# Ten rows of matmuls on a constant tile, put between TensorE's steps in the head of a linear-attention and two-stage expert kernel

## The chip, the cores and the metric

The kernel runs on one core of a Trainium2 chip. The metric is the device time of one execution in microseconds (us). The kernel before took 744.25 us, the median of three executions (742.01 to 744.28).

## The reference: what is computed

Three stages follow one another. First comes a linear attention over q, k, v of shape (8, 8, 576, 64):

```python
q_s = softmax(q, axis=-1)          # over the 64 columns of a head
k_s = softmax(k, axis=2)           # over the 576 positions
kv  = einsum('bhsd,bhse->bhde', k_s, v)
x   = einsum('bhsd,bhde->bhse', q_s, kv)       # then 4608 tokens of 512
h   = x @ w_in;  g = h / (1 + exp(-h));  x = g @ w_out
logits = x @ phi                    # 32 slots
slot_input = softmax(logits, axis=0).T @ x
slot_out   = 8 small two-layer networks on 4 slots each
out        = softmax(logits, axis=1) @ slot_out
```

Inputs are float32 here or are brought to it. The second line group has a hidden size of 2048, the last networks one of 1024.

## The kernel before

The 4608 tokens are cut into 18 chunks of 256. For each chunk the kernel builds x (tiles `x`, `x_mm`, lines 331 to 354), multiplies it with `w_in` in eight steps of 48 matmuls (`gemm1`, line 432, tiles `h`), forms the gated hidden tile (`act_u`) and gathers logits and slot sums. Each float32 product is made of a high and a low half: three matmuls on float32r operands replace one.

The work of the four compute engines is set out by hand. Strings of step names, `START` for the head, `CHUNK` for the middle and `END` for the tail, are played by `play`: each name runs one piece of a generator up to its next `yield`, and the instructions issued there go to the end of the queue of their engine. An engine works through its queue strictly in that order. The steps that matter here are `lq` and `qs` (loading and softmax of q: VectorE reduces a row, a matmul with the constant `swap` exchanges halves, VectorE reads the product, lines 276 to 304), `km`, `kT`, `ks`, `ke` and `kv` (the softmax of k and the products k·v: reduce, transpose on TensorE, lines 193 to 210, broadcast by a matmul with `ones`, tile `mb`, line 222, subtract, exponent, 20 matmuls, line 241), `w` and `p` (turning the loaded weights into float32 and its halves; VectorE at lines 387 and 388, VectorE or GpSimd at line 161), and `qT` and `x`. A star after a name hands a piece from GpSimd to VectorE.

TensorE's small products go to PSUM tiles with the tag `ps`, four buffers used in turn (pool `ps_s`). The tiles with tag `u0` come from the pool `cv_p` with six buffers. Two constants matter: `ident`, the identity, built by GpSimd at the start, and `swap`, which VectorE copies out of it (lines 711 and 712).

Of the kernel before, what the change touches and what calls it, by code (L numbers as in the profile page):

```python
# [8 lines left out]
F32 = mybir.dt.float32  # L9
F32R = mybir.dt.float32r  # L10
# [10 lines left out]


START = """
lq.0 lk.0.0 qs.0 qs.0 qs.0 qs.0 km.0 kT.0 qs.0 kT.0 kT.0 qs.0 lk.1.0 lw.0 km.1 qs.0 ks.0 kT.1 qs.0 w.0 ks.0
qs.0 kT.1 ke.0 qT.0.0 kT.1 lw.1 ks.1 qT.0.0 qT.0.0 w.1 w.0 w.0 ks.1 lphi lk.0.1 lk.1.1 lw.2 kv.0 qT.0.1 ke.1
w.1 w.0 lq.1 kv.1 w.2 qT.0.1 w.1 kv.0 w.0* qs.1 qT.0.1 w.1 kv.0 lw.3 lk.3.0 w.1 w.2 qs.1 lw.4 qs.1 kv.0 kv.1
w.2 kv.1 w.3 kv.1 km.3 kT.3 w.3 x.0.0 qs.1 w.2 x.0.1 x.0.0 w.4 w.3 w.2 x.0.1 kT.3 kT.3* x.0.0 lw.5 qs.1 w.3
w.4 lp.0 w.5 x.0.1 ks.3 qs.1 w.4 h.0.0 ks.3 w.3 w.5 h.0.1 qs.1 w.4 h.0.0 h.0.0 qs.1 w.4* w.5 h.0.2 qs.1 p.0
h.0.1 w.5 lp.1 lk.3.1 p.1 h.0.2 ke.3 lw.6 p.0 h.0.3 w.5 qT.1.0 h.0.1 h.0.4 p.0 lw.7 p.0 p.1 h.0.2 w.6 w.6 p.1
lp.2 qT.1.0 w.7 h.0.4 h.0.3 p.0 w.7 kv.3 p.1 h.0.5 qT.1.0 w.6 p.0 x.1.0 w.6 p.1 qT.1.1 p.1 h.0.3 h.0.4 p.0 p.1  # L30
w.7 kv.3 w.6* h.0.5 qT.1.1 w.7 x.1.0 l.0.1 h.0.6 lk.2.0 p.2 km.2 qT.1.1 x.1.0 p.2 kT.2 w.7 h.0.5 h.0.7 x.1.1
lp.3 p.2 kT.2 kT.2 p.2 kv.3 h.0.6 p.3 h.0.7 x.1.1 p.3 x.1.1 h.0.6 p.2 lp.4 lk.2.1 p.2 h.1.0 ks.2 p.4 lp.5 lq.2
h.0.7 kv.3 p.3 p.3 lp.6 p.4 p.5 p.3 h.1.0 p.4 p.5 h.1.1 p.3 h.1.2 qs.2 p.2 p.4 qs.2 ks.2 p.6 p.4 lp.7 p.3 qs.2
p.5 ke.2 l.0.3 p.4 h.1.0 p.5 h.1.1 p.5 p.7 qs.2 p.6 h.1.3 h.1.2 qs.2 h.1.3 p.6 h.1.1 p.4 p.7 p.5 kv.2 kv.2
p.7* h.1.4 p.6 p.5 qs.2 p.6* h.1.2 p.7 l.0.5 qs.2 p.6 h.1.5 qs.2 qs.2 p.7* kv.2 h.1.4 h.1.3 p.6 rg.0 p.7 h.1.6
p.7 qT.2.0 l.0.7 kv.2 h.1.4 h.1.5 qT.2.0 rg.0 qT.2.0 x.2.0 dl.0 x.2.0 dl.0 qT.2.1 h.1.5 rg.0 qT.2.1 qT.2.1
h.1.7 ds.0 ds.0 x.2.0 ds.0 x.2.1 l.1.1 dT.0 l.1.3 rg.0 x.2.1 h.1.7 h.1.6 dT.0 x.2.1 h.1.6 dg.0 dg.0 h.1.7 lq.3
lk.4.0 lk.4.1 l.1.5
"""
CHUNK = """  # L40
qs rg km h.0 h.0 o h.1 qs e.7 rg h.1 dl kT o h.0 kT sc sc kT* dl qs qs* h.1 h.2 rg ks ds h.3 ks ds qs h.2 h.3
# [22 lines left out]
def kernel(  # L64
# [19 lines left out]
    nc = tc.nc  # L84
# [3 lines left out]
    NS = phi.shape[1]  # L88
    E, F = w1.shape[1], 2 * w1.shape[3] // (phi.shape[0] // 128)
    SPE = NS // E  # L90
    P = 128
    CH = 256
# [23 lines left out]
    ident = const.tile([P, P], F32, name="ident")  # L116
# [13 lines left out]
    def ps(shape, name):  # L130
        cnt[0] += 1
        return ps_s.tile(shape, F32, tag="ps", name=f"{name}_{cnt[0]}")


    def right(name, bufs):
        st = ExitStack()
        return st.enter_context(tc.tile_pool(name=name, bufs=bufs, side="right")), st
# [12 lines left out]
    cv_p, cv_st = right("cv_p", 3)  # L150
# [158 lines left out]
    def warm_up(n, at):  # L309
        t = ps([P, P], "warm")  # L310
        for _ in range(n):
            nc.tensor.matmul(t, ident, ident, start=True, stop=True)


    def q_trans(c, half):
# [46 lines left out]
    def load_piece(kind, j):  # L362
        if j % 2 == 0:
            pool = {"w2": gb_p, "p0": gk_p, "p2": gk_p, "p6": gk_p}.get(f"{kind}{j}", ga_p)
            t = pool.tile([P, 2, KD * 256], w_in.dtype, tag="g", name=f"raw_{kind}{j}")
            for i in range(2):
                raw[kind, j + i] = t[:, i].rearrange("p (k f) -> p k f", k=KD)
        src = w_in if kind == "w" else w_out_t
        nc.sync.dma_start(raw[kind, j], src[j])
# [218 lines left out]
    def one(f):  # L588
        def g(*a):
            f(*a)  # L590
            return
            yield
        return g
# [61 lines left out]
    def close(st, n):  # L655
        st.close()
        give_slots(n)

    parts = {
        "wu": one(warm_up), "lq": one(load_q), "lk": one(kv_dma), "lphi": one(phi_dma),  # L660
        "lw": one(lambda j: load_piece("w", j)), "lp": one(lambda j: load_piece("p", j)),
        "km": one(kv_max), "kT": kv_maxT, "ks": kv_sub, "ke": one(kv_exp), "kv": kv_mm,
        "qs": q_soft, "qT": q_trans, "x": x_mm, "w": conv_w, "p": conv_p,
# [118 lines left out]
    for ft in range(KF):  # L782
        g = ft % G
        nc.tensor.matmul(psi[NS * g:NS * g + NS, :], aT[:, ft, :], w_t[ft // 4][:, ft % 4, :],
                         start=(ft < G), stop=(ft >= KF - G))
# [95 lines left out]
    for e in range(E):  # L881
        layer2(1, e)
        n = NCH * (e + 1) // E
# [59 lines left out]
```

## Time and profile before

| what | us |
|---|---|
| three executions | 742.01, 744.25, 744.28 |
| span of the profiled execution, first to last instruction | 741.5 |
| what an execution adds around the span (fastest and slowest run less the span) | 0.5 to 2.8 |
| TensorE busy in the span | 674.9 |
| VectorE busy in the span | 569.3 |
| ScalarE and GpSimd busy | 285.7 and 154.2 |

The profile gives the span of the profiled execution and no other time for it. Averages hide that the program has stages: in the first hundred microseconds VectorE is the busy engine and TensorE has gaps, later it is the other way round. Busy time of TensorE counts overlapping matmuls once, and the ends of matmuls are modelled; the distance between two starts is the safer price. A wait is read from the idle time in front of an instruction and from what ended it. The granted clock is a share of full speed: 1.00 is 2.4 GHz, 0.50 is 1.2 GHz.

### The profile page before, as it was taken

Reading aid. Unit: us, or ns where it says so; the run is one execution under the profiler, and the core shown is the slowest. Engines: PE = TensorE matmul, PEld = TensorE weight load, DVE = VectorE, ACT = ScalarE, POOL = GpSimd, SP = SyncE. Lnnn points to the kernel's source line nnn. Section 1 sums busy time; section 2 is a strip of 40 time slices with the busy share of each in tenths; the row PEclk is TensorE's granted clock in tenths of the full one; section 3 lists DMA queues with packets and bytes.
Section 4 is the critical chain, followed back from the end, with each engine's and each line's share of the span. In section 5 each row is a group of like instructions: output and inputs, shape, how many; then the busy total and the mean of one; then the engine's idle time right before and its main releaser. Section 6 shows DMA issues by size and latency. Waiting matters only on the chain.

```text
span 741.5 us, 15214 instructions
## 1 busy us (share of the span) xinstructions
PE 674.9 (91%) x6214; PEld 574.7 (77%) x6214; DVE 569.3 (77%) x998; ACT 285.7 (39%) x512; POOL 154.2 (21%) x108
## 2 busy tenths in 40 slices
PE   1347699999999999999999999999999999998993
PEld 1247588889897987989798898989898998893452
DVE  8999999788887979798888778878896784334253
ACT  3466564233444344333434334242433323322223
POOL 4857564011202111122112111010201000003000
PEclk9759799999999999999999999999999999999998
DMA  8623733665565739374765626845351747799998
GB/s 344 276 108 114 304 138 79 187 192 122 161 151 168 199 117 234 99 223 96 204 158 170 143 60 183 264 136 129 102 114 41 217 93 242 265 357 374 369 374 340
DMA packets 39509, 141.73 MB, mean 191 GB/s; under 512 B 6672, under 2 KB 6672, under 8 KB 30736
## 3 DMA queue, kind: packets, MB, share of 16 engines
q1 hardware_dynamic: 39440, 140.76, 60.4%
q8 instruction: 49, 0.80, 0.5%
q14 instruction: 20, 0.16, 0.1%
HBM read 93.55 MB, written 13.63 MB: 145 GB/s over the span
## 4 chain that ended last, share of the span: by engine, by line
PE 71%; DVE 17%; SPq 3%; issue 3%; ACT 2%; DMA 2%; POOL 0%; DVEq 0%; POOLq 0%; ACTq 0%
PE h L432 45%; PE sg L554 5%; PE pl L481 5%; SPq L491 3%; PE l L833 2%; DMA gk<-gT 2%; PE l L806 2%; PE kv L241 2%; DVE mg_p L388 2%; DVE mg_w L388 1%; PE x L348 1%; PE x L349 1%; DVE u L445 1%; PE x L347 1%; PE po L855 1%
## 5 line engine op out<-in xcount | busy, mean ns | idle before, releaser
L432 PE MATMUL h<-x,win_hi 128*128 128x256 f32 x2304 | 432.4, 289 | 5.0 <-DVE u L445 4.1
L432 PEld LDWEIGHTS h<-x,win_hi 128*128 128x128 f32 x2304 | 362.3, 194 | 32.7 <-issue 30.4
L432 PE MATMUL h<-x,win_lo 128*128 128x256 f32 x1152 | 328.1, 285 | 2.0 <-DVE win_lo L161 2.0
L432 PEld LDWEIGHTS h<-x,win_lo 128*128 128x128 f32 x1152 | 222.9, 193 | 2.3 <-DVE win_lo L161 2.3
L443 ACT ACTIVATE u<-h 128x512 f32<-128x512 f32 x144 | 85.5, 596 | 181.6 <-PE h L432 175.7
L445 DVE SCALAR_TENSOR_TENSOR u<-u,h 128x512 f32<-128x512 f32 x144 | 97.1, 674 | 51.0 <-ACT u L443 50.9
L452 DVE STREAM_TRANSPOSE gT<-u 128x512 f32<-128x512 f32 x128 | 91.1, 712 | 4.5
L161 POOL TENSOR_TENSOR q<-q,qsm 128x1024 f32<-128x1024 f32 x16 | 31.6, 1977 | 173.0 <-DVE qsm L303 76.8
L481 PE MATMUL pl<-u,wphi 128*32 128x256 f32 x576 | 47.5, 394 | 2.7 <-DVE wphi L419 2.7
L554 PE MATMUL sg<-gk,d 128*32 128x512 f32 x288 | 40.5, 594 | 1.8 <-DMA gk<-gT 1.4
L354 DVE TENSOR_TENSOR x<-x,x 128x512 fp32r<-128x512 f32 x36 | 24.7, 686 | 22.0 <-ACT x L352 21.5
L161 POOL TENSOR_TENSOR qlo<-q,qhi 128x512 fp32r<-128x512 f32 x17 | 22.5, 1322 | 90.6 <-ACT qhi L329 90.6
L294 ACT ACTIVATE q<-q 128x1024 f32<-128x1024 f32 x18 | 19.1, 1060 | 52.9 <-DVE q L161 48.9
L193 DVE TENSOR_REDUCE m<-kv 128x256 f32<-128x1280 f32 x16 | 39.3, 2454 | 0.0
L352 ACT CAST x<-x 128x512 fp32r<-128x512 f32 x36 | 21.0, 584 | 42.5 <-PE x L349 42.2
L161 POOL TENSOR_TENSOR mg_o<-mg_o,raw_o 128x512 f32<-128x512 f32 x16 | 20.9, 1308 | 73.3 <-DVE mg_o L388 64.8
L257 ACT CAST kvn_hi<-kvtmp 64x128 fp32r<-64x128 f32 x32 | 9.5, 296 | 51.2 <-DVE kvtmp L252 50.8
L329 ACT CAST qhi<-q 128x512 fp32r<-128x512 f32 x34 | 20.9, 615 | 18.9 <-DVE q L323 13.3
L348 PE MATMUL x<-qlo,kvn_hi 128*128 128x256 f32 (+3 forms) x96 | 27.3, 285 | 0.0
L349 PE MATMUL x<-qhi,kvn_lo 128*128 128x256 f32 (+3 forms) x96 | 27.2, 284 | 0.0
L347 PE MATMUL x<-qhi,kvn_hi 128*128 128x256 f32 (+3 forms) x96 | 27.2, 283 | 0.0
L554 PEld LDWEIGHTS sg<-gk,d 128*32 128x32 f32 x288 | 12.1, 109 | 18.7 <-issue 11.8
(155 smaller groups left out, 905.6 us busy)
## 6 DMA issues: line engine op xcount, KB each, us to landing
gk<-gT SPq DMA_DIRECT2D x256, 128.0 KB, 2.5
w<-in_moe_w_dram SPq DMA_DIRECT2D x32, 1024.0 KB, 7.5
kv<-in_kv_dram SPq DMA_DIRECT2D x16, 650.0 KB, 6.2
kv<-in_kv_dram SPq DMA_DIRECT2D x16, 640.0 KB, 4.9
q<-in_q_dram SPq DMA_DIRECT2D x18, 512.0 KB, 3.5
raw_w<-in_moe_w_in_dram SPq DMA_DIRECT2D x8, 1024.0 KB, 7.4
raw_p<-in_moe_w_out_t_dram SPq DMA_DIRECT2D x8, 1024.0 KB, 7.9
raw_o<-in_moe_w_out_dram SPq DMA_DIRECT2D x8, 1024.0 KB, 6.9
```

What stands on the lines that cost most here:

```text
L161: (nc.vector if star[0] else nc.gpsimd).tensor_tensor(*a)
L193: nc.vector.tensor_reduce(m1.rearrange("p (h d) -> p h d", h=HH), k_t[u].rearrange("p h j d -> p h d j"), axis=AX.X, op=ALU.max,)
L347: nc.tensor.matmul(o, kh, qh[:, i, p0:p1], start=True, stop=False)
L348: nc.tensor.matmul(o, kh, ql[:, i, p0:p1], start=False, stop=False)
L349: nc.tensor.matmul(o, kl, qh[:, i, p0:p1], start=False, stop=True)
L354: nc.vector.tensor_tensor(lo, px, hi.bitcast(F32), ALU.subtract)
L432: nc.tensor.matmul(ph[:, i, :], a, x[:, kk, :], start=(n == 0), stop=(n == 3 * KD - 1))
L443: nc.scalar.activation(u, ph, AF.Tanh, scale=0.5)
L445: nc.vector.scalar_tensor_tensor(u, u, 1.0, ph, ALU.add, ALU.mult)
L452: nc.vector.transpose(out=gT_t[c][:, :, 2 * s:2 * s + 2, :].rearrange("p j a f -> p a j f"), in_=u.rearrange("p a (j t) -> p a j t", t=32),)
L481: nc.tensor.matmul(pl_t[c][NS * g:NS * g + NS, :], wphi[:, ft, :], u[:, i, :], start=(ft < G), stop=(ft >= KF - G))
L554: nc.tensor.matmul(pg[NS * i:NS * i + NS, :], d[:, j, :], gk[:, j, i, :], start=(j == 0), stop=(j == TPC - 1))
```

## The change

A step `rw` (function `row`) is added. The first call fills two tiles of the tag `u0` with the identity, by eight copies on ScalarE. Every call takes two `ps` tiles and issues 16 matmuls on these constants into them; nothing reads the products. The ten rows differ in shape, and each stands once in `START`. Nothing else in the table changes its order; `CHUNK` and `END` are unchanged.

```diff
-lq.0 lk.0.0 qs.0 qs.0 qs.0 qs.0 km.0 kT.0 qs.0 kT.0 kT.0 qs.0 lk.1.0 lw.0 km.1 qs.0 ks.0 kT.1 qs.0 w.0 ks.0
+rw.0 lq.0 lk.0.0 qs.0 qs.0 qs.0 qs.0 km.0 kT.0 qs.0 rw.1 kT.0 kT.0 qs.0 lk.1.0 lw.0 km.1 qs.0 rw.2 ks.0 kT.1
...
+    shapes = {}
+
+    def row(n):
+        if not shapes:
+            for w in range(2):
+                t = cv_p.tile([P, 2, CH], F32R, tag="u0", name=f"row{w}", bufs=6)
+                for i in range(2):
+                    nc.scalar.copy(t[:, i, 0:P], ident)
+                    nc.scalar.copy(t[:, i, P:], ident)
+                shapes[w] = t
+        a, b = shapes[0], shapes[1]
+        f = a.rearrange("p i n -> p (i n)")
+        g = b.rearrange("p i n -> p (i n)")
+        o = [ps([P, 512], f"row{n}{x}") for x in range(2)]
+        mm = nc.tensor.matmul
+        for k in range(16):
+            t = o[k // 8]
+            m, w = (f, g)[k % 2], (a[:, 0, 0:P], a[:, 1, 0:P], b[:, 0, 0:P])[k % 3]
+            c = slice(NS * (k % 4), NS * (k % 4) + NS)
+            if n == 0:
+                mm(t, w, m, start=True, stop=True)
+            elif n == 1:
+                mm(t[:, 0:256], w, m[:, 0:256], start=True, stop=True)
+            elif n == 2:
+                mm(t, w, (a, b)[k % 2].rearrange("p i (x y) -> p x i y", x=2)[:, :, :, 0:P], start=True, stop=True)
+            elif n == 3:
+                mm(t[:, 0:384], w, m[:, 0:384], start=True, stop=True)
+            elif n == 4:
+                mm(t[c, :], w.bitcast(F32)[:, 0:NS], m.bitcast(F32), start=True, stop=True)
+            elif n == 5:
+                mm(t[c, 0:256], w.bitcast(F32)[:, 0:NS],
+                   m.bitcast(F32).rearrange("p (x y) -> p x y", y=64)[:, :, 0:32], start=True, stop=True)
+            elif n == 6:
+                mm(t[0:64, :], w[:, 0:64], m, start=True, stop=True)
+            elif n == 7:
+                mm(t[c, 0:256], w.bitcast(F32)[:, 0:NS], m.bitcast(F32)[:, 0:256], start=True, stop=True)
+            elif n == 8:
+                mm(t, f[:, 0:P], m, start=True, stop=True)
+            elif n == 9:
+                h = slice(64 * (k % 2), 64 * (k % 2) + 64)
+                mm(o[k % 2], w[h], m[h], start=True, stop=True)
```

On TensorE's queue the head of the kernel before begins as follows (`qmx` and `qsm` belong to `qs`, `m1T` to `kT`, `mb` to `ks`; 0 and 1 in these names are the first two halves of batch 0, and the numbers at the end count tiles).

```order
L286 MATMUL qmx_194<-qmx_192,swap 128x32
L204 MATMUL m1T_200<-ident,m_0_198 128x128 x2
L300 MATMUL qsm_222<-qsm_214,swap 128x32
L222 MATMUL mb_224<-dg_209,ones 128x256 x2
L204 MATMUL m1T_227<-ident,m_1_220 128x128 x2
L222 MATMUL mb_253<-dg_247,ones 128x256 x2
L241 MATMUL kv_270<-kv_190 64x65 x20
```

The same place in the changed kernel, with the first matmul of each row (`row` tiles; 15 more of the same shape follow each of them):

```order
L335 MATMUL row_1_198<-row_188 128x512
...
L286 MATMUL qmx_222<-qmx_220,swap 128x32
L204 MATMUL m1T_228<-ident,m_0_226 128x128 x2
L337 MATMUL row_5_232<-row_188 128x256
...
L300 MATMUL qsm_268<-qsm_260,swap 128x32
L339 MATMUL row_8_270<-row_188 128x512
...
L222 MATMUL mb_288<-dg_255,ones 128x256 x2
L204 MATMUL m1T_291<-ident,m_1_266 128x128 x2
L343 MATMUL row_12_301<-row_188 32x512
...
L350 MATMUL row_14_335<-row_188 32x256
...
L222 MATMUL mb_353<-dg_329,ones 128x256 x2
L345 MATMUL row_17_357<-row_188 32x256
...
L348 MATMUL row_19_388<-row_188 64x512
...
L241 MATMUL kv_406<-kv_218 64x65 x20
```

Every matmul of the softmax steps keeps its place among the others, and rows 0, 1, 2, 4, 7, 5 and 6 (in this order) stand in front of `qmx`, `qsm`, `mb`, `mb` and `kv`. Further down on TensorE, row 3 stands between the first and the second `kv`, and row 9 and row 8 stand as here, ahead of the first matmuls of `x`:

```order
L241 MATMUL kv_455<-kv_262 64x65 x20
L355 MATMUL row_25_491<-row_188 128x512
...
L286 MATMUL qmx_517<-qmx_487,swap 128x32
L204 MATMUL m1T_539<-ident,m_3_537 128x128 x2
L352 MATMUL row_29_544<-row_188 128x512
...
L390 MATMUL x_564<-qhi_0_325,kvn_hi_158 128x256
L391 MATMUL x_564<-qlo_0_326,kvn_hi_158 128x256
```

On ScalarE the queue of the changed kernel begins with the copies (before, it began with the table load and the exponent of q at line 294):

```order
L322 ACT_TABLE_LOAD
L322 CAST row_188<-ident 128x128
L323 CAST row_188<-ident 128x128
...
L294 ACTIVATE q_216<-q_216 128x1024
L427 ACTIVATE mg_w_296<-raw_w_264 128x1024
```

The two tiles of the tag `u0` are the first of their pool; the copies stand ahead of all other work of ScalarE.

## Rows read from the trace of the kernel before

**Rows 1.** The page: the span and the number of instructions.
```profile
span 741.5 us, 15214 instructions
```

**Rows 2.** Busy time per engine (count), granted clock, DMA share and rate, by stretch.
```profile
0.00:20.00 20.00, 3.79 (x11) 2.29 (x11) 16.78 (x38) 7.46 (x8) 10.46 (x21) 1.00 0.81 319
20.00:40.00 20.00, 5.47 (x83) 4.81 (x83) 18.41 (x21) 9.73 (x13) 15.85 (x8) 0.71 0.79 317
...
20.90:25.95 5.05, 4.48 (x81) 4.02 (x80) 4.78 (x5) 3.34 (x4) 3.17 (x2) 1.00 0.32 80
```

**Rows 3.** Pieces of the chain that ended last: start, length, engine, what.
```profile
121.30 1.14 DVE qsm L297
123.44 3.10 PE h L432 x24
...
157.44 1.32 PE kv L241 x40
...
259.30 1.72 PE sg L554 x16
```

**Rows 4.** TensorE in order of time: start, length, instruction, idle time before it.
```profile
6.69 0.64 PE L286 MATMUL qmx<-qmx,swap 128*128 128x32 f32 x2 [6.69 <-DVE qmx L283]
...
13.10 0.77 PE L222 MATMUL mb<-dg,ones 128*128 128x256 f32 x2
...
21.03 2.44 PE L241 MATMUL kv<-kv 128*64 128x65 f32 x40
...
42.66 0.41 PE L348 MATMUL x<-qlo,kvn_hi 128*128 128x256 f32 x1
...
44.80 0.41 PE L349 MATMUL x<-qhi,kvn_lo 128*128 128x256 f32 x1
```

**Rows 5.** Two stretches of `h` matmuls, columns as in Rows 2.
```profile
52.40:55.65 3.25, 3.15 (x14) 3.15 (x15) 3.25 (x4) 1.05 (x1) 3.25 (x2) 0.50 0.00 0
55.65:58.99 3.34, 3.34 (x28) 3.34 (x28) 3.31 (x3) 2.64 (x3) 1.30 (x2) 0.96 0.00 0
```

**Rows 6.** VectorE in order of time, at the instructions that need `ident` or TensorE.
```profile
1.34 2.07 DVE L711 COPY s<-ident 32x32 f32<-32x32 f32 x4 [1.34 <-POOL ident masks.py:199]
...
15.25 1.43 DVE L225 TENSOR_TENSOR kv<-kv,mb 128x1280 f32<-128x1280 f32 x1
...
21.14 1.49 DVE L225 TENSOR_TENSOR kv<-kv,mb 128x1280 f32<-128x1280 f32 x1 [0.93 <-PE mb L222]
...
25.80 0.15 DVE L249 TENSOR_SCALAR rz<-kv 128x2 f32<-128x2 f32 x1
...
34.41 0.17 DVE L288 TENSOR_TENSOR qmx<-qmx,qmx 128x32 f32<-128x32 f32 x1
...
49.30 0.68 DVE L354 TENSOR_TENSOR x<-x,x 128x512 fp32r<-128x512 f32 x1
```

**Rows 7.** ScalarE in order of time: the table load and the first cast of `x`.
```profile
4.32 1.28 ACT L294 ACT_TABLE_LOAD   x1 [4.32 <-DMA q<-in_q_dram]
...
43.97 0.59 ACT L352 CAST x<-x 128x512 fp32r<-128x512 f32 x1 [2.21 <-PE x L349]
```

**Rows 8.** Groups by line and shape: a 128x128 cast on ScalarE; busy us, mean ns.
```profile
L749 ACT CAST cc<-logit 128x128 fp32r<-128x128 f32 x1 | 0.3, 298 | 0.5 <-PE l L806 0.5
```

**Rows 9.** A GpSimd instruction, and two of VectorE, in order of time.
```profile
26.01 2.38 POOL L161 TENSOR_TENSOR mg_w<-mg_w,raw_w 128x1024 f32<-128x1024 f32 x1 [1.94 <-ACT win_hi L399]
...
26.39 3.09 DVE L161 TENSOR_TENSOR win_lo<-mg_w,win_hi 128x1024 fp32r<-128x1024 f32 x1
...
57.32 1.22 DVE L388 SCALAR_TENSOR_TENSOR mg_w<-raw_w,mg_w 128x1024 uint32<-128x1024 uint32 x1
```

**Rows 10.** VectorE's groups by line and shape, 26 to 124 us.
```profile
L388 DVE SCALAR_TENSOR_TENSOR mg_p<-raw_p,mg_p 128x1024 uint32<-128x1024 uint32 x8 | 14.0, 1754 | 0.3
L388 DVE SCALAR_TENSOR_TENSOR mg_w<-raw_w,mg_w 128x1024 uint32<-128x1024 uint32 x6 | 12.4, 2074 | 0.2
...
L161 DVE TENSOR_TENSOR win_lo<-mg_w,win_hi 128x1024 fp32r<-128x1024 f32 x3 | 8.4, 2804 | 0.0
```

More of the change, by code (lines that the diff above doesn't have):

```diff
@@ L23 @@
 START = """
-lq.0 lk.0.0 qs.0 qs.0 qs.0 qs.0 km.0 kT.0 qs.0 kT.0 kT.0 qs.0 lk.1.0 lw.0 km.1 qs.0 ks.0 kT.1 qs.0 w.0 ks.0
[L25 to L38, printed above, removed]
+rw.0 lq.0 lk.0.0 qs.0 qs.0 qs.0 qs.0 km.0 kT.0 qs.0 rw.1 kT.0 kT.0 qs.0 lk.1.0 lw.0 km.1 qs.0 rw.2 ks.0 kT.1
@@ new lines @@
+qs.0 w.0 ks.0 qs.0 rw.4 kT.1 ke.0 qT.0.0 kT.1 lw.1 rw.7 ks.1 qT.0.0 rw.5 qT.0.0 w.1 w.0 w.0 ks.1 lphi lk.0.1
+lk.1.1 lw.2 rw.6 kv.0 qT.0.1 ke.1 w.1 w.0 lq.1 rw.3 kv.1 w.2 qT.0.1 w.1 kv.0 w.0* qs.1 qT.0.1 w.1 rw.9 kv.0 lw.3
+lk.3.0 w.1 w.2 qs.1 lw.4 qs.1 kv.0 kv.1 w.2 kv.1 w.3 kv.1 km.3 kT.3 w.3 rw.8 x.0.0 qs.1 w.2 x.0.1 x.0.0 w.4 w.3
+w.2 x.0.1 kT.3 kT.3* x.0.0 lw.5 qs.1 w.3 w.4 lp.0 w.5 x.0.1 ks.3 qs.1 w.4 h.0.0 ks.3 w.3 w.5 h.0.1 qs.1 w.4
+h.0.0 h.0.0 qs.1 w.4* w.5 h.0.2 qs.1 p.0 h.0.1 w.5 lp.1 lk.3.1 p.1 h.0.2 ke.3 lw.6 p.0 h.0.3 w.5 qT.1.0 h.0.1
@@ new lines @@
+h.0.4 p.0 lw.7 p.0 p.1 h.0.2 w.6 w.6 p.1 lp.2 qT.1.0 w.7 h.0.4 h.0.3 p.0 w.7 kv.3 p.1 h.0.5 qT.1.0 w.6 p.0 x.1.0
+w.6 p.1 qT.1.1 p.1 h.0.3 h.0.4 p.0 p.1 w.7 kv.3 w.6* h.0.5 qT.1.1 w.7 x.1.0 l.0.1 h.0.6 lk.2.0 p.2 km.2 qT.1.1
+x.1.0 p.2 kT.2 w.7 h.0.5 h.0.7 x.1.1 lp.3 p.2 kT.2 kT.2 p.2 kv.3 h.0.6 p.3 h.0.7 x.1.1 p.3 x.1.1 h.0.6 p.2 lp.4
+lk.2.1 p.2 h.1.0 ks.2 p.4 lp.5 lq.2 h.0.7 kv.3 p.3 p.3 lp.6 p.4 p.5 p.3 h.1.0 p.4 p.5 h.1.1 p.3 h.1.2 qs.2 p.2
+p.4 qs.2 ks.2 p.6 p.4 lp.7 p.3 qs.2 p.5 ke.2 l.0.3 p.4 h.1.0 p.5 h.1.1 p.5 p.7 qs.2 p.6 h.1.3 h.1.2 qs.2 h.1.3
@@ L39 @@
+p.6 h.1.1 p.4 p.7 p.5 kv.2 kv.2 p.7* h.1.4 p.6 p.5 qs.2 p.6* h.1.2 p.7 l.0.5 qs.2 p.6 h.1.5 qs.2 qs.2 p.7* kv.2
+h.1.4 h.1.3 p.6 rg.0 p.7 h.1.6 p.7 qT.2.0 l.0.7 kv.2 h.1.4 h.1.5 qT.2.0 rg.0 qT.2.0 x.2.0 dl.0 x.2.0 dl.0 qT.2.1
+h.1.5 rg.0 qT.2.1 qT.2.1 h.1.7 ds.0 ds.0 x.2.0 ds.0 x.2.1 l.1.1 dT.0 l.1.3 rg.0 x.2.1 h.1.7 h.1.6 dT.0 x.2.1
+h.1.6 dg.0 dg.0 h.1.7 lq.3 lk.4.0 lk.4.1 l.1.5
 """
@@ L659 @@
     parts = {
-        "wu": one(warm_up), "lq": one(load_q), "lk": one(kv_dma), "lphi": one(phi_dma),
+        "wu": one(warm_up), "rw": one(row), "lq": one(load_q), "lk": one(kv_dma), "lphi": one(phi_dma),
         "lw": one(lambda j: load_piece("w", j)), "lp": one(lambda j: load_piece("p", j)),
```

## The prediction

> **What bounds the kernel now.** I read the busy time by stretch first. In the first 20 us VectorE is busy 16.78 us and TensorE 3.79, in the next 20 us 18.41 and 5.47 [rows 2]: the head hangs on VectorE, and TensorE has 40 − 9.26 = 30.7 us without work in it. The chain that ended last says the same: its pieces are VectorE's up to the reduce at 121.30, and from 123.44 on they are TensorE's `h` matmuls [rows 3]. So what delays VectorE in the first 123 us delays the end one for one, since behind it TensorE works without a gap. What delays TensorE alone in the head costs nothing until VectorE waits for a product. VectorE asks TensorE at few places: at 7.4 us (`qmx`, whose matmul starts at 6.69 [rows 4]), at 15.25, 21.14, 25.80, 34.41 and, by way of ScalarE's cast, at 49.30 [rows 6]. I therefore went through TensorE's queue row by row and asked at each of these places how late the product comes.
>
> **Prices of the rows.** No row's shape is in the trace; the nearest are these. A 128x256 matmul on float32r follows the last one after (44.80 − 42.66)/10 = 0.214 us at the lower clock [rows 4], and after 3.34/28 = 0.119 us at a granted clock of 0.96 [rows 5]. That is by columns, so 16 matmuls of 512 columns (rows 0, 2, 6, 8, 9) take 6.9 us at the lower level and 3.8 us at the upper, 256 columns (row 1) 3.4 and 1.9, 384 (row 3) 5.1 and 2.9. Plain float32 into 32 partitions is like `sg`: 16 records, two for each of 8 matmuls of 512 columns, in 1.72 us at the upper level [rows 3]; so 3.4 us for row 4 (6.9 at the lower level), and half of that for rows 5 and 7. Together 31 us at the upper and 57 us at the lower level: even at the upper level they fill the whole idle time of 30.7 us, so they can't all be hidden.
>
> **Which clock.** The granted clock reads 1.00 from 20.90 to 25.95 [rows 2], but the 40 matmuls of `kv` in it take 2.44 us [rows 4], where later 40 take 1.32 [rows 3]. The early reading is not what the matmuls show; I take the lower level for the start. From 52.40 the `h` matmuls ran without a gap at 0.50 until 55.65, and then at 0.96 [rows 5]; so a burst from rest is priced with half of its matmuls at each level, 8 × 0.428 + 8 × 0.239 = 5.3 us for 512 columns. From row 1 on TensorE hardly rests until row 9, and I take the upper level there.
>
> The Trainium skill (TensorE: Matmul & The Clock Gate, Part 1) says that the halved clock is the default and that activity lifts it; by that the early 1.00 is an unset reading. This trace's 2.44 us agrees. By the reading alone the first term below would be 2.1 instead of 3.6.
>
> **The sum, place by place.** All times are of the profiled execution; a delay, once there, moves everything behind it.
> - Row 0. It needs `ident` (1.34 us [rows 6]), the table load (1.28 us [rows 7]), which no longer waits for q, and eight casts of 128x128 at 0.30 us [rows 8]: ready at 5.0. With 5.3 us of matmuls TensorE is free at 10.3, where `qmx` now starts at 6.69: **+3.6**. Bounds: 3.8 us of matmuls gives +2.1, 6.9 gives +5.2. The casts themselves are hidden: ScalarE's next piece of work waits for `qmx`.
> - Row 1 stands before `qsm`, while VectorE does two reduces of k and one of q: 1.9 to 3.4 us beside them, **0** (1 at most).
> - Row 2 stands before `mb`. That matmul starts at 13.10, takes 0.77 [rows 4] and is read at 15.25 [rows 6], so 1.4 us are to spare. 3.8 us push it from 12.9 to 16.7, its end to about 17.3: **+2.0** (lower level: +5.1).
> - Rows 4 and 7, 5.1 us, stand before the second `mb`. TensorE reaches it at about 22.5 on the scale of the trace plus 3.6, ends it at 22.9, and VectorE wants it at 21.14 + 2.0: **0** (lower level +5).
> - Rows 5 and 6, 5.5 us, stand before `kv`, which takes 1.3 and some 0.2 to be seen: 29.9, wanted at 25.80 + 2.0 = 27.8: **+2.1** (lower level +8).
> - Row 3, the second `kv` and row 9 take 2.9 + 1.3 + 3.8, then `qmx` 0.65: 38.5, wanted at 34.41 + 4.1 = 38.5: **0**. If row 9's matmuls, which use 64 rows each in turn, run in pairs, 1.9 us are to spare; at the lower level +6.
> - Row 8 stands before `x`, after a rest of TensorE of some 8 us, so 5.3 us: the cast of `x` on ScalarE (0.59 us at 43.97 [rows 7]) comes at 49.3 with half a microsecond of matmul time won back at the upper level, and VectorE's line 354 wants it done at 49.30 [rows 6]. Behind the cast ScalarE has the next weight conversions, for which VectorE waits next: **+0.7** (lower level +2.7, nothing if the clock is already up).
>
> Sum: 3.6 + 2.0 + 2.1 + 0.7 = **+8.4 us** of waits on VectorE.
>
> **What comes back.** VectorE's `win_lo` takes 3.09 us from 26.39, and ends 1.1 us after a GpSimd instruction that ran from 26.01 to 28.39 [rows 9]; it was held up for 1.9 us. In the changed kernel VectorE stands at 25.80 for 2.1 us, GpSimd's instruction does not, and `win_lo` finds it finished: −1.9. More of this kind lies behind it: line 388 takes 1.22 us when nothing is in its way [rows 9], but 1.754 and 2.074 us on the mean over 14 cases, and `win_lo` 2.804 over three [rows 10]. That is 8 × 0.53 + 6 × 0.85 + 3 × 1.6 = 14.2 us of hold-ups up to 124 us. When VectorE's waits move it against GpSimd, some go and others come; I take another −0.8.
>
> The Trainium skill (SBUF — State Buffer, SBUF: two separate sides) says that VectorE and GpSimd share a pair of ports as an exclusive lock, held for the whole instruction, so the later one fully blocks. The trace's 3.09 us agrees. Without that rule the sum would stay at 8.4.
>
> Net **+5.7 us**: the span of 741.5 [rows 1] becomes 747.2, and with 0.5 to 2.8 us around it 747.7 to 750.0. Against the median of the runs, which lies 2.75 above that span, it is 744.25 + 5.7 = **750.0 us**.
>
> **DMA.** The transfer of the third half batch into the buffer of the first waits for `kv`, which ends some 8 us later than now, while the reader is some 5 us later; I see no reader that comes to wait, and price it at nothing.
>
> **Rivals.**
> - *A shape that is dearer than its columns.* Rows 2 and 5 read their moving operand in pieces, row 6 has 64 columns of weights, row 9 half of the rows. For it: no such shape is in the trace. Against it: `kv` with 64 columns and `sg` with 32 cost what their columns say. If row 2 or row 6 costs double, its 3.8 us come on top at a place where no slack is left, and row 5 another 1.7: +9 to +13, about 755 us.
> - *The clock stays at the lower level through the head.* The rests of VectorE's chain between the rows speak for it, the 31 us of rows in 30.7 us against it. The lower prices above give 5.2 + 5.1 + 5 + 8 + 6 + 2.7 = 32, less 2.7 that come back: about 773 us.
> - *Not slower: the hold-ups between VectorE and GpSimd come back in full.* Place: VectorE's lines 388 and 161 from 26 to 124 us; price: up to 14.2 us. For it: VectorE is the bound there, and each hold-up depends on who starts first. From the point at which 6.2 of the 14.2 us are saved, the sum falls below 2.2 us; with 8.4 it is zero, and with 10 it would be 742.6. Against it: most hold-ups are between instructions that feed one another, and move together.
> - *The rows cost nothing because nothing reads them.* They stand in TensorE's queue ahead of `qmx`, `mb` and `kv`, so only row 0's lateness could shrink, to +2.1; this is inside the case before.
>
> **How the numbers follow.** What a measurement of this kernel can tell from no change is 0.3%, 2.2 us. The forecast (+3 to +8.5; 747.5 to 753) has 0.68. Dearer shapes 0.13, the clock staying low 0.05. The hold-ups coming back 0.14: 0.09 of it within 2.2 us, 0.03 faster, 0.02 still slower. So slower 0.88, same 0.09, faster 0.03. The range of 745 to 758 leaves out the low clock and the far ends of the others.
>
> **What would show it.** `qmx` starts near 10.3 and not 6.69; VectorE is idle before lines 288, 225 (first) and 249 for 3 to 4, 2 and 2 us; rows 1, 4, 7, 3 and 9 end before VectorE asks. `win_lo` at 26.39 + delay takes about 1.2 us. The last VectorE piece of the chain comes at 127 instead of 121. I am wrong if one row takes over 5.5 us behind row 1, if VectorE's idle time in the head is far from 8 us, or if the same waits are seen and the `h` matmuls of the middle nevertheless start on time.

## The result and the profile after

The changed kernel takes 747.14 us, the median of eight executions (744.94 to 750.46), against 742.45 us of the kernel before, eight executions beside them (740.64 to 744.28). The ratio is 1.0062, 95% interval 1.0038 to 1.0086: 4.7 us slower. (One execution of e5 below, of 1314 us, is left out of its ratio and its median.) The profiled execution took 746.72 us, 1.8 us more than its span, which answers to [rows 1]:

```profile
span 744.9 us, 15643 instructions
```

TensorE in the head, in order of time (start, length, instruction, idle time before it). These are the first matmuls of rows 0, 1, 2, 5, 6, 9 and 8, the last three of row 0, and the products that stand behind the rows ([rows 4] has those of before).

```profile
2.97 0.79 PE L335 MATMUL row<-row 128*128 128x512 f32 x1 [2.97 <-ACT row L323]
...
8.81 0.86 PE L335 MATMUL row<-row,row 128*128 128x512 f32 x3
9.51 0.30 PE L286 MATMUL qmx<-qmx,swap 128*128 128x32 f32 x2
...
12.75 0.56 PE L337 MATMUL row<-row 128*128 128x256 f32 x1
...
15.88 0.30 PE L300 MATMUL qsm<-qsm,swap 128*128 128x32 f32 x2
16.02 0.47 PE L339 MATMUL row<-row 128*128 128x512 f32 x1
...
19.78 0.41 PE L222 MATMUL mb<-dg,ones 128*128 128x256 f32 x2
...
26.06 0.40 PE L345 MATMUL row<-row 128*32 128x256 f32 x1
...
27.93 0.45 PE L348 MATMUL row<-row 128*64 128x512 f32 x1
...
31.75 1.39 PE L241 MATMUL kv<-kv 128*64 128x65 f32 x40
...
37.40 0.49 PE L355 MATMUL row<-row 64*128 64x512 f32 x1
...
39.45 0.41 PE L286 MATMUL qmx<-qmx,swap 128*128 128x32 f32 x2
...
48.78 0.78 PE L352 MATMUL row<-row 128*128 128x512 f32 x1
...
54.44 0.28 PE L390 MATMUL x<-qhi,kvn_hi 128*128 128x256 f32 x1
```

The distance from a row's first matmul to what stands behind it (for row 5 that is row 6) is the row's price: row 0 6.5 us, row 1 3.1, row 2 3.76, row 5 1.9, row 6 3.8, row 9 2.05, row 8 5.7. The clock that goes with them, by stretch (columns as in [rows 2]):

```profile
3.00:8.40 5.40, 5.40 (x12) 3.96 (x13) 2.70 (x13) 0.72 (x4) 0.56 (x2) 1.00 1.03 416
8.40:12.00 3.60, 1.41 (x8) 1.07 (x6) 2.15 (x2) 0.00 (x0) 1.88 (x1) 0.99 0.98 401
12.00:15.00 3.00, 2.56 (x12) 2.59 (x13) 2.09 (x5) 2.90 (x3) 1.13 (x5) 0.50 1.08 423
15.00:20.00 5.00, 5.00 (x28) 4.33 (x27) 2.90 (x4) 0.37 (x1) 2.30 (x3) 0.97 0.56 230
20.00:40.00 20.00, 19.86 (x232) 12.43 (x230) 15.77 (x20) 10.78 (x12) 13.77 (x10) 1.00 0.51 190
40.00:45.00 5.00, 0.00 (x0) 0.00 (x0) 4.82 (x6) 0.05 (x1) 4.07 (x2) 0.77 1.00 423
45.00:50.00 5.00, 1.53 (x5) 1.37 (x6) 4.62 (x5) 3.74 (x5) 0.00 (x0) 0.50 0.59 245
```

Row 0's matmuls show the lower level up to about 8.4 us, whatever the reading says (its first 13 take 5.84 us, 0.45 each), and the upper one for its last three (0.23 each, from 8.81 to 9.51). TensorE then rests until 12.4 us and is at the lower level again for most of row 1. From 15 to 40 us it is at the upper level, falls back while it rests between rows 9 and 8, and has to be brought up again by row 8. VectorE, at the instructions of [rows 6] and [rows 9]:

```profile
9.85 0.19 DVE L288 TENSOR_TENSOR qmx<-qmx,qmx 128x32 f32<-128x32 f32 x1 [4.07 <-PE qmx L286]
...
20.23 1.49 DVE L225 TENSOR_TENSOR kv<-kv,mb 128x1280 f32<-128x1280 f32 x1 [2.29 <-PE mb L222]
...
26.17 1.49 DVE L225 TENSOR_TENSOR kv<-kv,mb 128x1280 f32<-128x1280 f32 x1 [1.13 <-PE mb L222]
...
33.19 0.16 DVE L249 TENSOR_SCALAR rz<-kv 128x2 f32<-128x2 f32 x1 [2.44 <-PE kv L241]
...
33.79 1.86 DVE L161 TENSOR_TENSOR win_lo<-mg_w,win_hi 128x1024 fp32r<-128x1024 f32 x1
...
39.89 0.19 DVE L288 TENSOR_TENSOR qmx<-qmx,qmx 128x32 f32<-128x32 f32 x1 [0.19 <-PE qmx L286]
40.00 4.22 DVE L260 TENSOR_TENSOR kvn_lo<-kvtmp,kvn_hi 64x128 fp32r<-64x128 f32 x2
...
55.97 0.69 DVE L397 TENSOR_TENSOR x<-x,x 128x512 fp32r<-128x512 f32 x1
```

The three waits that the prediction named are there. The first, 4.07 us, is longer than the delay that it makes: 0.73 us of it are there before the change too, and 0.9 us come from q's first reduce, which began at 4.56 us in this execution and at 5.42 us in that of before. VectorE is late by 2.5 us at the first of these instructions, by 5.0 at 20.23, still 5.0 at 26.17 (rows 4 and 7 are hidden), 7.4 at 33.19 and 6.7 at 55.97. The chain of waits then passes to TensorE ([rows 3]):

```profile
128.43 1.14 DVE qsm L297
130.58 3.10 PE h L475 x24
...
166.43 1.73 PE sg L597 x16
...
365.03 1.88 PE sg L597 x10
```

The first two pieces are 7.1 us later than before. The span is only 3.4 us longer, so 3.7 us come back between 130 us and the end. The chain of the kernel before shows where:

```profile
160.20 1.88 PE sg L554 x10
...
287.23 6.89 DMA gk<-gT
294.21 1.88 PE sg L554 x10
```

`sg` forms the slot sums of the chunk before (line 554, `slot_g`), whose operand `gk` is brought by 16 transfers, the gathers, on SyncE's queue (`regroup`). Its 8 matmuls leave 16 records. A group "x10" in this chain is one in which the last ten of them stood until a transfer had landed. The kernel before has four, at 160, 227, 294 and 362 us; the changed kernel has one, at 365 us. In the groups by line the 288 records and the idle time ahead of them read, before and after:

```profile
L554 PE MATMUL sg<-gk,d 128*32 128x512 f32 x288 | 40.5, 594 | 1.8 <-DMA gk<-gT 1.4 <-DVE d L545 0.3
```

```profile
L597 PE MATMUL sg<-gk,d 128*32 128x512 f32 x288 | 38.0, 593 | 0.4 <-DVE d L588 0.3
```

That is 42.3 against 38.4 us, 3.9 less. Between the `u` activations at 136.9 and 664.5 us of before, and the same two of the changed kernel, all other groups of matmuls agree to 0.2 us, so what comes back in the middle comes back at `sg`. To follow the delay along the run I compared the start of the same `u` activation of ScalarE (before: line 443) in each profile with that in the first profile of before. All numbers are us; the first column is the time in before, the last two are span and median.

| kernel | 137 | 194 | 261 | 363 | 665 | span | median |
|---|---|---|---|---|---|---|---|
| changed, first profile | +7.1 | +6.1 | +5.2 | +3.5 | +3.0 | +3.4 | 747.14 |
| changed, second profile (e8) | +7.9 | +6.8 | +5.6 | +4.6 | +4.4 | +5.0 | 747.54 |
| e1, hidden rows alone | +1.1 | +1.8 | +0.9 | +0.8 | +1.8 | +1.8 | 743.12 |
| e2, rows in TensorE's rests | -0.3 | -1.2 | -1.9 | -3.1 | -3.0 | -3.0 | 741.45 |
| e3, row 0 alone, 36 matmuls | +6.3 | +5.8 | +4.6 | +4.3 | +2.8 | +5.6 | 748.52 |
| e4, before again | +0.5 | +1.6 | +0.7 | +0.4 | +0.8 | +1.3 | 743.15 |
| e5, exposed rows alone | +8.1 | +7.2 | +6.6 | +5.3 | +4.2 | +4.7 | 749.94 |
| e6, before, `sg` later | 0.0 | -0.7 | -1.8 | -3.0 | -2.8 | -2.5 | 740.68 |
| e7, changed, `sg` later | +7.9 | +7.3 | +6.2 | +5.1 | +5.0 | +5.3 | 748.09 |

The kernel before ran 742.82 us beside e1 to e4 and 743.32 us beside e5 to e8 (medians of 29 and 11 executions).

### The profile page after: what moved, and what is told of

Its sections match the earlier page's. It is cut to its first block, busy times and chain, and to the rows that moved or that the text cites. A ratio compares the mean times of both kernels' runs of the same rounds, so it can differ in the third digit from the quotient of the medians.

```text
span 744.9 us, 15643 instructions
## 1 busy us (share of the span) xinstructions
PE 702.0 (94%) x6422; PEld 595.6 (80%) x6422; DVE 567.4 (76%) x998; ACT 287.1 (39%) x520; POOL 154.0 (21%) x108
## 4 chain that ended last, share of the span: by engine, by line
PE 82%; DVE 13%; ACT 2%; issue 2%; DMA 0%; SPq 0%; DVEq 0%; ACTq 0%
PE h L475 49%; PE pl L524 5%; PE sg L597 5%; PE kv L241 2%; PE l L876 2%; PE l L849 2%; DVE mg_p L431 2%; PE po L898 2%; PE x L391 1%; PE x L392 1%; PE x L390 1%; DVE mg_p L430 1%; DVE u L488 1%; PE uT L508 1%; DVE m L193 1%
## 5 line engine op out<-in xcount | busy, mean ns | idle before, releaser
L597 PE MATMUL sg<-gk,d 128*32 128x512 f32 x288 | 38.0, 593 | 0.4 <-DVE d L588 0.3
L366 DVE STREAM_TRANSPOSE q<-q 128x512 f32<-128x512 f32 x34 | 23.6, 693 | 3.4 <-POOL q L161 3.4
```

The costliest lines, as they stand in the source:

```text
L597: nc.tensor.matmul(pg[NS * i:NS * i + NS, :], d[:, j, :], gk[:, j, i, :], start=(j == 0), stop=(j == TPC - 1))
```

## The experiments

**e1: the hidden rows alone.** Rows 0, 2, 5 and 6 are without their matmuls; row 0 only fills the tiles.

```diff
-        for k in range(16):
+        for k in range(0 if n == 0 else 16):
...
-... qs.0 rw.2 ks.0 kT.1 ... qT.0.0 rw.5 qT.0.0 ... lw.2 rw.6 kv.0
+... qs.0 ks.0 kT.1 ... qT.0.0 qT.0.0 ... lw.2 kv.0
```

> Rows 1, 4, 7, 3, 9 and 8 stay where the change puts them; rows 0, 2, 5 and 6 have no matmuls, and the two constant tiles are still filled at the start. Theory (only rows that VectorE waits for cost something): the first h matmul of the PE-bound stretch, at 123.44 us before and 130.58 with all ten rows, comes at 123.5 to 126 (0 to 2.5 later; 0.7 of it for row 8, up to 1.5 if row 4 runs at the lower clock because row 2 no longer precedes it), and the time is 0 to 2.5 us above before. Rival (TensorE's total work in the head counts, wherever it stands): these six rows are 15.5 of the 30 us of matmuls, so about half of the 7.1, 3.5 us, with VectorE's idle time spread over all of its reads.

743.12 us, ratio 0.9997 [0.9979, 1.0014]. The 96 matmuls more on TensorE's queue cost nothing that can be measured. VectorE is on time to 0.1 us at the first `kv`, and 0.5 us late behind row 8. Compared with the changed kernel this puts the 4.7 us on rows 0, 2, 5 and 6. The waits at `sg` are as before (40.1 and 3.0 us, 43.1 in all).

**e2: all ten rows, moved to where TensorE rests.** The tiles are filled at the start; rows 0, 2, 5, 6 and 8 stand behind the products that they had delayed, row 4 behind the second `kv`, and row 9 ahead of the next q step.

```diff
-rw.0 lq.0 ... qs.0 rw.2 ks.0 ... rw.5 qT.0.0 ... lw.2 rw.6 kv.0 ... rw.8 x.0.0
+rw.10 lq.0 ... qs.0 ks.0 ... qT.0.0 ... lw.2 kv.0 ... rw.9 qs.1 rw.0 rw.2 rw.5 ... x.0.1 rw.6 x.0.0 ... rw.8 h.0.3
```

> All ten rows with their 160 matmuls, but row 0, 2 and 5 moved into TensorE's rest after the second qmx, row 4 behind the second kv, row 6 behind the matmuls of x and row 8 ahead of the fourth h step; rows 1, 7, 3 and 9 near their old places. Theory (place decides): the first h matmul of the PE-bound stretch comes at 123 to 125 instead of 130.58, and the time is 0 to 1.5 us above before. Rival (the amount of work counts): the same +7 us at that matmul and +4.7 us in time as with the rows in their first places.

741.45 us, ratio 0.9984 [0.9971, 0.9997]: the same 160 matmuls, and no time for them. VectorE at the same places as above:

```profile
6.50 0.19 DVE L288 TENSOR_TENSOR qmx<-qmx,qmx 128x32 f32<-128x32 f32 x1 [0.73 <-PE qmx L286]
...
25.03 0.15 DVE L249 TENSOR_SCALAR rz<-kv 128x2 f32<-128x2 f32 x1
```

The cost of the change is a matter of place, not of work. In this execution too q's first reduce began at 4.56 instead of 5.42 us, which accounts for the small lead at the start. The lead grows from 0.3 to 3.0 us in the middle, and `sg` stands at 39.2 and 0.5 us, 39.7 in all: 2.6 less than before, in a kernel whose head is not late.

**e3: a single delay at the start.** Row 0 alone, with 36 matmuls.

```diff
-        for k in range(16):
-            t = o[k // 8]
+        for k in range(36):
+            t = o[k // 18]
...
-rw.0 lq.0 ... rw.1 ... rw.2 ... rw.4 ... rw.7 ... rw.5 ... rw.6 ... rw.3 ... rw.9 ... rw.8 ...
+rw.0 lq.0 ...
```

> Only row 0, but with 36 matmuls instead of 16; no other row. TensorE is then free for the first qmx at about 14.1 us instead of 9.5, so everything behind it is moved by 7.05 us at once and nothing else is changed. Theory A (a delay of the head reaches the end one for one, and the 3.7 us that the profiled run of the change won back between 161 and 367 us were transfers that happened to come late in the profiled run of before): first h matmul of the PE-bound stretch at 130.5, time 6 to 8 us above before. Theory B (a later head is partly won back in the middle, because the gathers of gk then meet fewer other transfers): the same 130.5, but only 3 to 5 us in time. Theory C (VectorE's hold-ups against GpSimd win back part of it already in the head): first h matmul before 129.

748.52 us, ratio 1.0085 [1.0068, 1.0101], 5.7 us slower by the medians and 6.3 by the ratio. VectorE's first wait is 7.39 us, the delay there +6.65, and the first `h` of the chain starts at 129.79, +6.35: through the head a delay at the start is handed on almost whole. Behind it 3.5 us come back by 665 us, and the tail takes 2.8 again. In the last 22 us of the span TensorE's clock reads 0.64, where before it reads 0.86 (first line before, second e3):

```profile
719.50:741.50 22.00, 10.76 (x80) 7.26 (x72) 8.41 (x13) 7.80 (x15) 0.00 (x0) 0.86 0.82 337
```

```profile
725.10:747.10 22.00, 10.13 (x44) 8.12 (x42) 7.35 (x11) 7.04 (x13) 0.00 (x0) 0.64 0.73 299
```

So the total came to the lower edge of the range expected for "one for one" (6 to 8 us), but by luck: a gain in the middle and a loss in the tail nearly cancelled. As many `sg` waits went as in the changed kernel (38.1 and 0.9 us, 39.0 in all). What lowers the clock in the tail was not tried.

**e4: the kernel before again,** for a second profile.

> The kernel before, unchanged, for a second profile. Theory A (late gathers come and go by chance): the waits of sg for gk near 160, 227 and 293 us are of other sizes than the 1.0, 1.0 and 1.9 us of the first profile, and the offset against the first profile moves in steps at these places; first h matmul of the PE-bound stretch within 0.5 us of 123.44. Theory B (they belong to the kernel): the same three waits within 0.2 us. Time 742.5 us within 0.2%.

743.15 us, ratio 1.0010 [0.9999, 1.0022]. Its `sg` group reads 40.0 and 2.7 us of idle time, 42.7 in all, and its chain has late groups at 161.78, 260.95 and 362.96, not all in the chunks of the first profile. In these two executions the waits differ in their place, and hardly in their sum.

**e5: the exposed rows alone.** Rows 0, 2, 5 and 6, without the six others.

```diff
-... qs.0 rw.1 kT.0 ... qs.0 rw.4 kT.1 ... lw.1 rw.7 ks.1 ... lq.1 rw.3 kv.1 ... w.1 rw.9 kv.0 ... w.3 rw.8 x.0.0
+... qs.0 kT.0 ... qs.0 kT.1 ... lw.1 ks.1 ... lq.1 kv.1 ... w.1 kv.0 ... w.3 x.0.0
```

> The changed kernel with rows 0, 2, 5 and 6 alone, the four that delayed VectorE; rows 1, 4, 7, 3, 9 and 8 are left out. Theory A: the hidden rows did something for the others, they kept TensorE busy so that rows 2, 5 and 6 ran at the upper clock level; without them row 2 starts on a rested engine, its 16 matmuls take 5 to 7 us instead of 3.7, rows 5 and 6 together more than 5.6, and VectorE is late by 8 to 11 us after the wait for kv, where the changed kernel had +7.4. Time 748 to 751. Rival B: the price of a row does not hang on the hidden ones; the delay after kv stays at +7.4, without row 8's half microsecond the first h that TensorE sets the pace for comes 6 to 7 us late, time 746 to 747.5.

749.94 us, the median of five, ratio 1.0085 [1.0066, 1.0105]. With 96 matmuls less than the changed kernel it is not faster; by the medians it is 2.4 us slower than e8, but the two intervals against the kernel before still touch. TensorE (rows 2, 5 and 6 and the products behind them), then VectorE, then the clock:

```profile
16.05 0.77 PE L339 MATMUL row<-row 128*128 128x512 f32 x1
...
21.46 0.40 PE L222 MATMUL mb<-dg,ones 128*128 128x256 f32 x2
...
27.54 0.63 PE L345 MATMUL row<-row 128*32 128x256 f32 x1
...
31.11 0.69 PE L348 MATMUL row<-row 128*64 128x512 f32 x1
...
35.91 2.55 PE L241 MATMUL kv<-kv 128*64 128x65 f32 x80
```

```profile
21.90 1.49 DVE L225 TENSOR_TENSOR kv<-kv,mb 128x1280 f32<-128x1280 f32 x1 [3.64 <-PE mb L222]
...
37.35 0.16 DVE L249 TENSOR_SCALAR rz<-kv 128x2 f32<-128x2 f32 x1 [4.94 <-PE kv L241]
```

```profile
15.00:20.00 5.00, 4.37 (x12) 3.59 (x13) 3.23 (x4) 0.69 (x1) 2.37 (x4) 0.54 0.58 240
```

Row 2 takes 5.4 us instead of 3.76, row 5 3.6 instead of 1.9, row 6 4.8 instead of 3.8, and VectorE is late by 11.5 us at line 249, where the changed kernel has 7.4. Theory A holds: the rows that are hidden kept the clock at the upper level, and so made the exposed ones cheap. In this profiled execution most of it comes back at once, at `win_lo` (1.69 us, [rows 9] has 3.09) and the instructions behind it: the first `h` of the chain is 8.1 us late, 0.2 to 1.0 more than in the changed kernel. This execution, of 748.02 us, is the fastest of the five; it ends 0.3 us before the span of e8, so where the others lose the 2.4 us was not seen. What e5 shows is the delay at `kv`, not a time that is longer beyond doubt.

**e6 and e7: `sg` one `h` step later,** in the kernel before and in the changed one. In the strings `sg` is the first `dg` of a chunk. An `h` step is 24 matmuls (`x24` in the chain), some 3 us: not 48 matmuls, as said of `gemm1` above, and not the 16 of 1.9 us of the expectation.

```diff
-... h.3 rg kv l.1 dg kv o sc qs qT.0 h.5 kv ow qT.0 h.4 ...
+... h.3 rg kv l.1 kv o sc qs qT.0 h.5 dg kv ow qT.0 h.4 ...
```

> The kernel before, with the step that multiplies the gathered slot sums (sg) put one h step of 16 matmuls (1.9 us) later in each middle chunk, and nothing else. Theory A: in the kernel before TensorE stands at sg for late gathers, 2 to 5 us in all in the two profiles so far, and this is what took up part of the changed kernel's delay; with the step later the waits are gone and the time is 739 to 741. Rival B: the gathers are not what moves; the lost time turns up at another step of the chunk and the time is 742 to 743.

> The changed kernel with the same edit of sg. Theory A: the changed kernel had next to no waits at sg left, so it gains little, 0 to 1 us (746 to 747), and its distance to the kernel before with the same edit is the whole delay of the head, 6 to 7 us. Rival B: both gain alike and the distance stays at 4.7 us.

e6 takes 740.68 us, ratio 0.9961 [0.9947, 0.9974], the fastest kernel here. e7 takes 748.09, ratio 1.0057 [1.0042, 1.0073], no faster than the changed kernel beside it (e8, 747.54). The groups by line of e6 and of e7:

```profile
L554 PE MATMUL sg<-gk,d 128*32 128x512 f32 x288 | 35.2, 597 | 0.3 <-DVE d L545 0.3
```

```profile
L597 PE MATMUL sg<-gk,d 128*32 128x512 f32 x288 | 35.3, 597 | 0.3 <-DVE d L588 0.3
```

35.5 and 35.6 us, and no idle time for a transfer, in either. (These sums can be held against each other, not against the ones above: `sg` now stands behind `h` matmuls, its records overlap with others, and e7's 3.3 us less than e8's bring it no time.) The two kernels then stay 7.9 us apart from 137 us (0.0 and +7.9 in the table) to 665 us (-2.8 and +5.0, that is 7.8), 7.8 in the spans and 7.4 in the medians. With the waits at `sg` out of the way the head's delay reaches the end whole; with them, 4.2 to 4.7 us arrive. The missing part is waits for `gk` that the kernel before has and the changed one has not: in that theory A holds for both. The head's delay as such need not be what removed them: e2, whose head is on time, lost 2.6 us of them, and e1 kept them all. Why fewer gathers are late in the changed kernel, whose chunks are the same, was not found: the late ones land after some 7 us, where the median is 2.5, and SyncE's queue carries a 1024 KB weight load between them in both kernels.

**e8: the changed kernel again.**

> The changed kernel without an edit, for a second profile and more runs. Theory A: the head repeats to 0.3 us (VectorE late by 2.5, 5.0 and 7.4 us at the first qmx, the first mb and kv; the first h that TensorE sets the pace for at 130 to 131), while the waits at sg differ by 1 to 3 us from those of the first profile; time 746.5 to 748. Rival B: sg has no waits again, so that they are a matter of the kernel and not of the execution.

747.54 us, ratio 1.0051 [1.0036, 1.0067]. The waits at `sg` are again small (38.4 and 0.5 us, 38.9 in all), so in two executions of each kernel they go with the kernel, and not with the one execution; theory A was wrong there. The head is 0.8 us longer than in the first profile, more than the 0.3 us I had allowed. VectorE is late by 2.9, 5.6 and 8.0 us at the three places: row 0 ran at the lower level almost to its end (6.95 us instead of 6.5). In e7, whose head has the same instructions, it is row 2 that runs in part at the lower level (the wait for `mb` is 3.79 us). The clock of 15 to 20 us, which reads 0.97 in the first profile, in e8 and then in e7:

```profile
15.00:20.00 5.00, 5.00 (x26) 4.42 (x26) 3.31 (x4) 0.79 (x1) 2.31 (x4) 0.88 0.56 228
```

```profile
15.00:20.00 5.00, 5.00 (x21) 4.31 (x20) 2.62 (x3) 0.16 (x1) 2.08 (x2) 0.67 0.56 230
```

With half speed until the rise and full speed behind it, that puts the rise at about 15.3, 16.2 and 18.3 us. So the price of the first rows depends on when the clock rises, and that moved by 3 us between executions of the same instructions. The Trainium skill (TensorE: Matmul & The Clock Gate, Part 1) says that this moment varies from run to run; these three profiles agree.

## Why the prediction was right

The forecast was 750.0 us in a range of 745 to 758, slower with 0.88: the time lies 2.9 us below it, and the sign and the range held. Of the 2.9 us, 1.8 are not the change's: the kernel before ran at 742.45 us this time and not at 744.25. The difference was forecast at +5.7 and is +4.7. The steps, in us:

| step | predicted | first profile | second (e8) |
|---|---|---|---|
| row 0, `qmx` | +3.6 | +2.5 | +2.9 |
| row 2, first `mb` | +2.0 | +2.5 | +2.7 |
| rows 4 and 7, second `mb` | 0 | +0.1 | +0.1 |
| rows 5 and 6, `kv` | +2.1 | +2.4 | +2.4 |
| row 8 and what comes back between VectorE and GpSimd | +0.7 - 2.7 | -0.3 | -0.1 |
| end of the head | +5.7 | +7.1 | +7.9 |
| `sg` in the middle | 0 | -4.1 | -3.5 |
| tail | 0 | +0.4 | +0.6 |
| span | +5.7 | +3.4 | +5.0 |

- *Where it costs.* Right, row by row. The waits before lines 288, 225 and 249 (4.07, 2.29 and 2.44 us) are those named, rows 1, 4, 7, 3 and 9 cost 0.2 us at most, and e1 and e2 show it from the other side.
- *Row 0.* Two errors of opposite sign. The casts took 0.29 us each, as in [rows 8], but one begins every 0.20 us, and the table load, which no longer waits for q [rows 7], began at 0.73:

```profile
0.73 1.28 ACT L322 ACT_TABLE_LOAD   x1 [0.73 <-PEq L975]
2.02 0.30 ACT L322 CAST row<-ident 128x128 fp32r<-128x128 f32 x1
2.23 0.29 ACT L323 CAST row<-ident 128x128 fp32r<-128x128 f32 x1
```

  So row 0 starts at 2.97 instead of 5.0 and need not wait for all eight. Its matmuls, mostly at the lower level, take 6.5 us and not 5.3: 13 of 16, and not half, came before the rise. The early clock reading of 1.00 is indeed not what the matmuls show.
- *Prices.* Right: 3.76 us for row 2 against 3.8, 3.8 for row 6, 1.9 for row 5. No shape was dearer than its columns; the rival of dearer shapes falls. Row 9's halves did run in pairs (2.05 us).
- *Which clock.* Right from row 2 to row 9; row 1, priced at 1.9 to 3.4 us, was still mostly at the lower level (3.1 us). That it depended on the hidden rows was said only in passing; e5 prices it at 4.1 us of delay at `kv` (3.5 against e8).
- *What comes back.* The size was off: 2.7 us were predicted. The mechanism at `win_lo` is there, 1.86 us instead of 3.09 (not the 1.2 forecast: GpSimd's next instruction, 1.30 us from 33.27, had begun before it), and at 39.89 VectorE had won back 1.9 of its 7.4 us. But the next instruction met GpSimd again: the pair of `kvn_lo` at 40.00 takes 4.22 us, beside two instructions of GpSimd,

```profile
39.78 2.37 POOL L161 TENSOR_TENSOR mg_w<-mg_w,raw_w 128x1024 f32<-128x1024 f32 x1 [1.89 <-DVE mg_w L431]
42.11 1.96 POOL L161 TENSOR_TENSOR q<-q,qmx 128x1024 f32<-128x1024 f32 x1
```

  and ends 0.15 us after the second; before, the pair took 2.67 us. Hold-ups were moved, not removed.
- *One for one to the end.* This step failed: "behind it TensorE works without a gap", and so a delay of VectorE delays the end one for one. TensorE does have gaps there, [rows 3] shows pieces of the chain only up to 259 us and I did not look at how `sg`'s groups were split. Against up to 4.1 us of the head's delay stand waits for gathers that the kernel before has and the changed one has not; why it has not stays open. Only e6 against e7, where those waits are gone, has the delay arriving whole. The prediction listed "the same waits, and the `h` matmuls of the middle start on time" as what would prove it wrong; they start 3.0 to 4.4 us late at the end of the middle instead of 7.1 to 7.9. The total came out near by luck: too small a head (+5.7 for +7.1) met waits of the kernel before that I had not seen.

## What to carry to other kernels

Work added to an idle engine is free exactly up to the slack of the product that stands behind it in that engine's queue; go through the queue place by place, and move the work behind the product rather than shrink it. Matmuls that are hidden can be worth having, since the exposed ones behind them run at the clock that they keep up. And before a delay is carried to the end, look in the chain of waits for steps that stand for a transfer: what they cost changed here by up to 4 us though nothing near them was touched, and giving such a step one step more of slack made the kernel before 2.6 us faster.

## What the runs showed of the hardware

- Matmuls on two halves of 64 rows, in turn into different tiles, ran two at a time: 16 of 512 columns in 2.05 us (row 9), against 3.76 with 128 rows at the same clock (row 2).
- A moving operand read in pieces of 128 or of 32 elements cost no more than a plain one: row 2 took 3.76 us, where 16 plain matmuls at row 8's last spacing of 0.23 us make 3.7; row 5 took 1.9 us, row 7, the same without pieces, 1.8.
- 64 columns of weights cost what 128 do: 3.8 us (row 6 against row 2's 3.76).
- ScalarE's 128x128 casts last 0.29 us each and start every 0.20 us: they overlap.
- The clock column reads 1.00 from the start, while row 0's matmuls of 512 columns follow one another every 0.43 us, the lower level; in the first profile reading and matmuls agree only from about 8.4 us on. In e4 the column reads 1.00 up to 60 us, and the `x` matmuls at 43 us follow one another every 0.21 us per 256 columns, the lower level too.
- TensorE's clock was down again when row 8 began, after 8.6 us in which TensorE waited for VectorE's reduce at line 193.
